# Attention over inducing points and a linearised feed-forward block: the instruction order as a table, with products and evictions moved between engines

## The chip, the cores and the metric

One core of a Trainium2 chip. The metric is device time in microseconds of one launch; the kernel before takes 184.81 us (median of 3 runs, 184.63 to 185.28). Engines: TensorE (PE; PEld is its weight load), VectorE (DVE), ScalarE (ACT), GpSimd (POOL) and SyncE (SP), whose queue issues every transfer.

## The reference

```python
def mab(q, kv):                       # x: 4 x 12480 x 128, inducing: 32 x 128, all float32
    s = (q @ kv.transpose(0, 2, 1)) / np.sqrt(C)
    s = s - s.max(-1, keepdims=True)
    a = np.exp(s)
    a /= a.sum(-1, keepdims=True) + 1e-09
    return a @ kv
h = mab(I, x)                         # 32 inducing points attend to a batch's 12480 tokens
y = mab(x, h).reshape(-1, 128)        # each token attends to the 32 rows of h
f = y @ w_in                          # 128 x 2048
out = (f - np.tanh(f)) @ w_out        # 2048 x 128
```

The inputs hold the two weights in 64 bits; the kernel brings them to 32 bits itself, from integer pieces.

## The kernel before, in words

**Batches and steps.** A batch of tokens is cut into 7 steps of 1792 tokens (the last overlaps the one before), and the steps into pairs 0-1, 2-3, 4-5 and 6. `first(b)` makes h of batch b:
- a *score step* (line 401, its matmuls on L378): four groups of 448 tokens against the inducing points, fp32, 8 matmuls. VectorE copies a pair's scores out of PSUM and takes their maximum (L405).
- the maximum over the batch (L418, L419, the product L421, L423), then per pair the exponential on ACT (L432) and a 32 x 32 block transpose on VectorE (L434).
- a *weighted sum* (L469): 14 chunks of the step against the tokens in natural layout. That layout is either loaded (`LOADED`, 13 steps of 28, L444) or made by TensorE in two *half transposes* (L454, 7 matmuls each) that ACT (L460) or VectorE (L462) copies out.
- the sums' inverse (L476 to L483), the scaling L485, and the product L487, which gives h transposed (copied by L490).

`linear(b)` replaces the feed-forward block by its tangent: h times w_in (line 505), transposed (L512), its mean over the 32 rows (L516, L517), tanh (L519), a short series of the mean on GpSimd (L525 to L530), the tangent (L535 to L539), the product with w_out (L548), and two small products (L554, L555). L561 (GpSimd) and L563 measure how far a row lies from the mean.

`second(b)` makes the outputs: scores against h (L378), the copy with the maximum (L592), one shift for each of two groups of pairs (L599 to L607), the exponential (L616), and per step an *output step* on TensorE (L631) whose two halves are evicted by ACT (L647) or VectorE (L649) and stored (L638). `bound()` (L672 to L738) decides at the end whether the tangent is good enough; if not, a general path runs, which it does not for these inputs.

**Weights.** `weight()` loads w_in and w_out in four chunks of 512 columns each (L336). A chunk takes four VectorE instructions (L339, L342, L353, L357), two on ACT (L346, L349) and a product on GpSimd (L360).

**Places.** All transfers land in 19 places of 128 x 1792 (`big`): token loads, natural layouts, weight chunks, outputs. PSUM gives three pairs of banks (`d`) for scores, transposes and outputs, and a `side` pair for small products, which one half of an output step uses too (`SIDE`).

**Order.** `Plan.add` records 584 operations with costs and priorities; `Plan.order` plays them through a list scheduler (engine costs, priorities with the hand-set offsets `JIT`, a switching cost on PE, tokens that limit how many places x and natural layouts hold) and writes the order of every engine's instructions. Evictions go to ACT or VectorE as the scheduler finds them free. On the chip each engine runs its list in that order and waits for what its next instruction needs; SyncE does so with its transfers.

Of the kernel before, what the change touches and what calls it, by code (L numbers as in the profile page):

```python
# [19 lines left out]
NQ = 4  # L20
# [16 lines left out]
JIT = {  # L37
# [28 lines left out]
}  # L66
SIDE = frozenset(((3, 3, 0),))
TOKENS = dict(x=14, nat=7)
LOADED = frozenset(((0, 6), (1, 1), (1, 2), (1, 4), (1, 6), (2, 1), (2, 3), (3, 0), (3, 1), (3, 3), (3, 4), (3, 5), (3, 6)))
RATE = 0.41  # L70
AHEAD = 5.0
LATE = 10.0
WAIT = -11.700000000000006
LOADW = (-31.5, -27.0)
PA, OT, PT, OB, PB = -8.0, 25.0, 11.0, -17.5, 16.0
LOADX, LOADN = 32, 313.5
SPLITS = ([[0, 1], [2, 3]], [[0], [1], [2], [3]], [[0, 1], [2], [3]], [[0, 1, 2, 3]], [[0, 1, 2], [3]], [[0], [1, 2, 3]])
SPLIT = (0, 4, 0, 0)
SWITCH = 12.5
PAUSE = 0.1  # L80


class Buf:


    def __init__(self, make=None, tag=None, token=None, turn=None):
        self.make, self.tag, self.token, self.turn = make, tag, token, turn
        self.t = None
        self.writer, self.readers, self.left = None, [], 0
        self.slot = None  # L90
# [7 lines left out]
class Op:  # L98
    def __init__(self, costs, fn, deps, bufs, pri, lag, size, mode):
        self.costs, self.fn, self.deps, self.bufs, self.pri, self.lag, self.size, self.mode = (  # L100
            costs, fn, deps, bufs, pri, lag, size, mode)
        self.start = self.end = self.eng = None


class Plan:


    def __init__(self, places):
        self.ops, self.places = [], places

    def add(self, eng, cost, fn, reads=(), writes=(), pri=0.0, lag=0.12, size=0, hold=(), mode=None):
        deps = set()
        for x in reads:
            if x.writer:
                deps.add(x.writer)
        for x in writes:
            if x.writer:
                deps.add(x.writer)
            deps.update(x.readers)
        costs = eng if isinstance(eng, dict) else {eng: cost}  # L120
        op = Op(costs, fn, deps, list(dict.fromkeys([*reads, *writes, *hold])), pri, lag, size, mode)
        for x in reads:
            x.readers.append(op)
        for x in writes:
            x.writer, x.readers = op, []
        for x in op.bufs:
            x.left += 1
        self.ops.append(op)
        return op

    def order(self):
        free = {tag: list(range(n)) for tag, n in self.places.items()}
        waiting, users = {}, {}
        for n, op in enumerate(self.ops):
            op.n = n
            waiting[op] = len(op.deps)
            for d in op.deps:
                users.setdefault(d, []).append(op)
        ready = {eng: [] for eng in ("ACT", "PE", "DVE", "POOL", "SP")}
        events, count = [], itertools.count()  # L140
        busy, turns = {}, {}
        mode = None
        moving = 0.0

        def release(op):
            for eng in op.costs:
                late = LATE if eng == "DVE" and len(op.costs) > 1 else 0.0
                ready[eng].append((op.pri + late, op.n, op))
                ready[eng].sort(key=lambda x: x[:2])

        for op in self.ops:
            if not op.deps:
                release(op)
        t, done = 0.0, 0
        while done < len(self.ops):
            for eng in ready:
                if busy.get(eng, -1.0) > t:
                    continue
                if eng == "SP" and moving > t + AHEAD:
                    heapq.heappush(events, (moving - AHEAD, next(count), None))  # L160
                    continue
                queue = ready[eng]
                if eng == "PE":
                    queue = sorted(queue, key=lambda x: (x[0] + (SWITCH if x[2].mode != mode else 0.0), x[1]))
                for _, _, op in queue:
                    if eng == "DVE" and len(op.costs) > 1 and busy.get("ACT", -1.0) < t + WAIT:
                        continue
                    new = [x for x in op.bufs if x.tag and x.slot is None]
                    need = {}
                    for x in new:  # L170
                        for tag in (x.tag, x.token):
                            if tag:
                                need[tag] = need.get(tag, 0) + 1
                    if any(len(free[tag]) < c for tag, c in need.items()):
                        continue
                    if any(x.turn is not None and turns.get(x.token, 0) != x.turn for x in new):
                        continue
                    for x in new:
                        x.slot = free[x.tag].pop(0)
                        if x.token:  # L180
                            free[x.token].pop()
                            turns[x.token] = turns.get(x.token, 0) + 1
# [20 lines left out]
            while events and events[0][0] <= t:  # L203
                op = heapq.heappop(events)[2]
                if op is None:
                    continue
# [16 lines left out]
def fused_kernel(ctx, tc, xT, xn, indT, w_in, w_out, outT):  # L223
# [5 lines left out]
    B = 4  # L229
# [262 lines left out]

# [357 lines left out]
```

## Time and profile before

| | |
|---|---|
| profiled execution | 184.3 us, span 182.3 us |
| PE busy | 152.7 us (84%), 1920 matmuls |
| DVE busy | 141.2 us (77%), 279 instructions |
| ACT busy | 96.0 us (53%), 141 instructions |
| POOL busy | 21.7 us (12%), 46 instructions |
| transfers | 67.76 MB, mean 372 GB/s; queue q1 93.2% of the 16 engines |

A share is an average over stages with different limits. A matmul's end is modelled, and a busy PE can be one that waits inside a group. SyncE's waits are waits of the queue's next transfer for a place or for the data it stores.

### The profile page before, as it was taken

Reading aid. Unit: us, or ns where it says so; the run is one execution under the profiler, and the core shown is the slowest. Engines: PE = TensorE matmul, PEld = TensorE weight load, DVE = VectorE, ACT = ScalarE, POOL = GpSimd, SP = SyncE. Lnnn points to the kernel's source line nnn. Section 1 sums busy time; section 2 is a strip of 40 time slices with the busy share of each in tenths; the row PEclk is TensorE's granted clock in tenths of the full one; section 3 lists DMA queues with packets and bytes.
Section 4 is the critical chain, followed back from the end, with each engine's and each line's share of the span. In section 5 each row is a group of like instructions: output and inputs, shape, how many; then the busy total and the mean of one; then the engine's idle time right before and its main releaser. Section 6 shows DMA issues by size and latency. Waiting matters only on the chain.

```text
span 182.3 us, 4643 instructions
## 1 busy us (share of the span) xinstructions
PE 152.7 (84%) x1920; PEld 85.4 (47%) x1920; DVE 141.2 (77%) x279; ACT 96.0 (53%) x141; POOL 21.7 (12%) x46
## 2 busy tenths in 40 slices
PE   0349797499999998999999999999999987899700
PEld 0019455197735574476277755535764323344200
DVE  4188999984479769788999775789988899896920
ACT  2255867841123279339435755295474752697600
POOL 1033333332005000000130000002200022000000
PEclk9999999759999999999999999999999999969955
DMA  5999999979999999899999999999999996489992
GB/s 153 348 422 425 415 410 420 373 269 337 409 423 426 414 421 333 286 422 412 368 352 419 426 416 427 418 370 350 421 419 425 423 405 276 204 351 401 400 399 75
DMA packets 11548, 67.76 MB, mean 372 GB/s; under 512 B 1408, under 2 KB 1408, under 8 KB 11520
## 3 DMA queue, kind: packets, MB, share of 16 engines
q1 hardware_dynamic: 11520, 67.39, 93.2%
q8 instruction: 17, 0.28, 0.6%
q14 instruction: 11, 0.09, 0.1%
HBM read 41.83 MB, written 25.56 MB: 370 GB/s over the span
## 4 chain that ended last, share of the span: by engine, by line
PE 69%; DVE 16%; DMA 5%; ACT 3%; issue 1%; SPq 1%; DVEq 0%; ACTq 0%
PE d L378 22%; PE side L469 14%; PE d L454 12%; PE d L631 11%; DMA big<-in_xT 5%; DVE big L649 4%; PE side L548 2%; PE side L378 2%; PE side L602 2%; ACT big L460 2%; DVE big L462 1%; DVE et L434 1%; DVE sl L405 1%; PE side L554 1%; PE side L487 1%
## 5 line engine op out<-in xcount | busy, mean ns | idle before, releaser
L647 ACT ACTIVATE big<-d,Pm,wg 128x896 f32<-128x896 f32 x28 | 30.3, 1093 | 20.4 <-PE d L631 15.5
L378 PE MATMUL d<-big,indT_sb 128*32 128x448 f32 x224 | 29.0, 586 | 12.2 <-DMA big<-in_xT 10.7
L649 DVE TENSOR_SCALAR big<-d,wg,Pm 128x896 f32<-128x896 f32 x27 | 32.5, 1204 | 3.8 <-PE d L631 2.1
L631 PE MATMUL d<-sl,k 32*128 32x448 f32 x220 | 33.3, 605 | 1.3 <-DVE all_far L563 0.8
L460 ACT COPY big<-d 128x896 f32<-128x896 f32 x22 | 19.4, 909 | 28.2 <-PE d L454 24.9
L469 PE MATMUL side<-big,et 128*32 128x128 f32 x784 | 30.7, 290 | 1.1 <-DVE et L434 1.0
L469 PEld LDWEIGHTS side<-big,et 128*32 128x32 f32 x784 | 24.9, 116 | 10.1 <-issue 4.7
L454 PEld LDWEIGHTS d<-ident,big 128*128 128x128 f32 x210 | 24.6, 149 | 10.4 <-issue 4.8
L454 PE MATMUL d<-ident,big 128*128 128x128 f32 x210 | 28.4, 289 | 0.2 <-ACT big L460 0.2
L378 PE MATMUL d<-big,hT 128*32 128x448 f32 x224 | 24.7, 542 | 0.6 <-DVE sl L592 0.6
L405 DVE TENSOR_SCALAR_CACHE_REDUCE sl<-d 128x896 f32<-128x896 f32 (+1 forms) x16 | 15.5, 970 | 5.8 <-PE d L378 5.7
L631 PEld LDWEIGHTS d<-sl,k 32*128 32x128 f32 x220 | 10.7, 187 | 15.1 <-ACT big L647 4.0
L592 DVE TENSOR_SCALAR_CACHE_REDUCE sl<-d 128x896 f32<-128x896 f32 (+1 forms) x16 | 15.4, 965 | 2.1 <-PE d L378 2.0
L434 DVE STREAM_TRANSPOSE et<-sl 128x896 f32<-128x896 f32 (+1 forms) x16 | 15.7, 984 | 1.0 <-issue 0.9
L616 ACT ACTIVATE sl<-sl,nbs 128x896 f32<-128x896 f32 (+1 forms) x16 | 15.0, 941 | 2.9 <-DVE nbs L605 2.9
L378 PEld LDWEIGHTS d<-big,indT_sb 128*32 128x32 f32 x224 | 6.9, 111 | 19.9 <-issue 10.1
L432 ACT ACTIVATE sl<-sl,nb 128x896 f32<-128x896 f32 (+1 forms) x16 | 15.0, 940 | 0.9 <-DVE nb L423 0.9
L378 PEld LDWEIGHTS d<-big,hT 128*32 128x32 f32 x224 | 7.0, 109 | 11.6 <-issue 7.0
L462 DVE COPY big<-d 128x896 f32<-128x896 f32 x8 | 8.5, 1086 | 3.0 <-PE d L454 2.3
L346 ACT ACTIVATE big<-big 128x512 f32<-128x512 uint32 x8 | 5.4, 688 | 7.6 <-DMA big<-in_w_in 7.6
L360 POOL TENSOR_TENSOR win_sb<-win_sb,big 128x512 f32<-128x512 f32 x4 | 5.6, 1392 | 18.5 <-DVE big L353 12.5
L339 DVE TENSOR_SCALAR big<-big 128x512 uint32<-128x512 uint32 x8 | 3.4, 420 | 5.2 <-DMA big<-in_w_in 5.2
(109 smaller groups left out, 136.4 us busy)
## 6 DMA issues: line engine op xcount, KB each, us to landing
big<-in_xT SPq DMA_DIRECT2D x28, 896.0 KB, 9.3
outT<-big SPq DMA_DIRECT2D x23, 896.0 KB, 6.7
big<-in_xn SPq DMA_DIRECT2D x13, 896.0 KB, 9.6
outT<-big SPq DMA_DIRECT2D x3, 864.0 KB, 9.7
big<-in_w_in SPq DMA_DIRECT2D x4, 512.0 KB, 8.4
big<-in_w_out SPq DMA_DIRECT2D x4, 512.0 KB, 14.5
outT<-big SPq DMA_DIRECT2D x3, 448.0 KB, 6.5
outT<-big SPq DMA_DIRECT2D x1, 416.0 KB, 4.7
```

What stands on the lines that cost most here:

```text
L378: nc.tensor.matmul(ps[q * m:(q + 1) * m, :n], lhsT=w, rhs=row, start=True, stop=True)
L405: nc.vector.tensor_scalar(out=sl.get()[:, :n, :], in0=ps.get()[:, :n, :W], scalar1=1.0, scalar2=None, op0=ALU.mult, op1=ALU.max, accum_out ...
L432: nc.scalar.activation(out=t, in_=t, func=AF.Exp, scale=SC, bias=nb.get(), accum_out=sums.get()[:, g:g + 1])
L434: add("DVE", 0.16 + 0.00103 * W * len(pair), lambda e, et=et, sl=sl, n=len(pair): nc.vector.transpose(out=et.get()[:, :n * KB, :].rearrang ...
L454: nc.tensor.transpose(out=o[:, k * 128:(k + 1) * 128], in_=x.get()[:, at:at + 128], identity=ident)
L460: nc.scalar.copy(out=dst, in_=src)
L469: nc.tensor.matmul(hacc.get()[q * m:(q + 1) * m, :C], lhsT=et.get()[:, j * KB + k, :], rhs=xn_t.get()[:, k * C:(k + 1) * C], start=at < NQ ...
L592: nc.vector.tensor_scalar(out=sl.get()[:, :n, :], in0=ps.get()[:, :n, :W], scalar1=1.0, scalar2=None, op0=ALU.mult, op1=ALU.max, accum_out ...
L616: nc.scalar.activation(out=t, in_=t, func=AF.Exp, scale=SC, bias=nb)
L631: nc.tensor.matmul(ds[q // 2].get()[:, q % 2, :W], lhsT=P4.get()[r, :], rhs=sl.get()[r, j, :], start=True, stop=True)
L647: nc.scalar.activation(out=dst, in_=src, func=AF.Identity, scale=wg.get(), bias=Pm.get())
L649: nc.vector.tensor_scalar(out=dst, in0=src, scalar1=wg.get(), scalar2=Pm.get(), op0=ALU.mult, op1=ALU.add)
```

## The change

The list scheduler goes. Its place takes a table, `ORDER`, of 584 words: an operation's number, the engine that runs it (P, A, D, G for GpSimd, S), and a letter for each place that it takes first. `order()` only reads it. Priorities, costs, `JIT` and tokens are gone. What differs in the instructions:
- 12 steps of natural layout are loaded instead of 13; `SIDE` has three halves instead of one.
- a weight chunk's product can run on VectorE or GpSimd; the table puts chunk 2 of w_in on VectorE, the seven others on GpSimd. L561 can run on either too: VectorE in batch 2.
- the series runs on VectorE, from the sum instead of the mean, in five instructions instead of six; the scaling of the mean (L517) goes from VectorE to ACT, and tanh scales its input itself.
- batch 1's pairs are split in two groups as 0-1, 2-3 and 4-5, 6 instead of three pairs and one.

```diff
-SIDE = frozenset(((3, 3, 0),))
+SIDE = frozenset(((3, 0, 1), (3, 3, 0), (3, 5, 1),))
-SPLIT = (0, 4, 0, 0)
+SPLIT = (0, 0, 0, 0)
+ORDER = """
+1G 2D 3D 70Sa 68Sb 97Pac 99Pb 100A 98D 75Sd 94Pae 95A 0S 20Sf 21D 4Sg 5D 7A 111Pbh 8A 69Pac 71P 6D 112D 22D 28Si 29D 24A 10D 73Sj 92Pa 9D 93A 109Pb
...
+577Pa 562S 570A 571S 578Da 579Pa 580Da 581Pa 582D 583D
+"""
     def order(self):
-        free = {tag: list(range(n)) for tag, n in self.places.items()}
...
+        for word in ORDER.split():
+            n, eng, slots = re.fullmatch(r"(\d+)([A-Z])([a-z]*)", word).groups()
+            op = self.ops[int(n)]
+            op.eng = next(x for x in op.eng.split("/") if x[0] == eng or (x, eng) == ("POOL", "G"))
+            new = [x for x in op.bufs if x.tag and x.slot is None]
+            for x, slot in zip(new, slots):
+                x.slot = ord(slot) - ord("a")
+            ops.append(op)
...
+            def scale(eng, r=r, dst=dst):
+                v = nc.gpsimd if eng == "POOL" else nc.vector
+                v.tensor_tensor(out=dst, in0=dst, in1=r["e"].bitcast(F32), op=ALU.mult)
+            add("POOL/DVE", scale, reads=[buf, ex], writes=[outs[k]])
...
+        def turned(e):
+            nc.vector.transpose(out=MT.get().rearrange("p f i -> p (f i)"), in_=psM.get())
+            nc.vector.tensor_reduce(out=total.get(), in_=MT.get(), axis=AX.X, op=ALU.add)
+        add("ACT", lambda e: nc.scalar.activation(out=th.get(), in_=total.get(), func=AF.Tanh, scale=1.0 / m),
+            reads=[total], writes=[th])
+        add("ACT", lambda e: nc.scalar.activation(out=mean.get(), in_=total.get(), func=AF.Copy, scale=1.0 / m),
+            reads=[total], writes=[mean])
         def series(e):
-            v = nc.gpsimd
+            v = nc.vector
+            a, q, y = u.get(), g.get(), total.get()
...
+            v.scalar_tensor_tensor(out=q, in0=q, scalar=c[0], in1=a, op0=ALU.add, op1=ALU.mult)
```

The table's lists, read off by engine (x12 is the token load of batch 1 step 2, n its natural layout, wi and wo chunks of w_in and w_out):

```
first transfers, before: ind x01 wi0 wi1 x00 wi2 x03 wi3 x02 x04 wo0 x05 wo1 x06 wo2 wo3 x12 n06 x10 x11 x15 x13 x14
first transfers, table:  x01 x00 x03 ind wi2 wi0 wi3 x02 x04 x05 x06 wo2 x11 x12 wo1 wi1 n05 x10 wo0 x13 wo3 x14 x15 x16
```

In the table VectorE's instructions between the last copy of batch 0's scores and the first transpose L434 are the maximum, L339 of one chunk, the shift and one copy of a half transpose; L353 and the product of chunk 2 of w_in stand ahead of that copy. After the last L487, VectorE has nine output evictions, and the part of `bound()` from L696 on stands behind the last of them; before it had eleven, and that part stood among the last four.

## Rows read from the trace of the kernel before

**Rows 1.** The page: transfer rate in 40 equal slices of the span.
```profile
GB/s 153 348 422 425 415 410 420 373 269 337 409 423 426 414 421 333 286 422 412 368 352 419 426 416 427 418 370 350 421 419 425 423 405 276 204 351 401 400 399 75
```

**Rows 2.** Busy time by stage: stage, length, PE, PEld, DVE, ACT, POOL, clock, DMA share, GB/s.
```profile
0.00:49.43 49.43, 34.55 (x395) 22.98 (x395) 35.42 (x70) 25.61 (x37) 11.93 (x15) 0.93 0.94 361
49.43:81.06 31.63, 30.79 (x443) 16.67 (x439) 25.50 (x55) 14.28 (x24) 2.59 (x9) 1.00 0.98 389
81.06:117.12 36.06, 35.70 (x481) 22.01 (x481) 30.01 (x52) 19.50 (x29) 2.35 (x7) 1.00 1.01 405
117.12:141.43 24.31, 24.13 (x372) 13.09 (x370) 21.07 (x43) 15.41 (x24) 2.47 (x8) 1.00 1.01 398
141.43:174.45 33.02, 27.56 (x240) 10.61 (x239) 29.19 (x62) 21.20 (x28) 2.35 (x7) 0.94 0.86 354
174.45:182.30 7.85, 0.00 (x0) 0.00 (x0) 0.00 (x0) 0.00 (x0) 0.00 (x0) 0.50 0.56 211
```

**Rows 3.** Instructions in time order, the first 14 us: start, duration, what, [idle before].
```profile
6.12 1.72 PE L378 MATMUL d<-big,indT_sb 128*32 128x448 f32 x8 [6.12 <-DMA big<-in_xT]
8.13 0.43 DVE L339 TENSOR_SCALAR big<-big 128x512 uint32<-128x512 uint32 x1 [5.17 <-DMA big<-in_w_in]
...
11.62 1.72 PE L378 MATMUL d<-big,indT_sb 128*32 128x448 f32 x8 [3.78 <-DMA big<-in_xT]
...
12.88 0.68 ACT L346 ACTIVATE big<-big 128x512 f32<-128x512 uint32 x1 [1.49 <-DMA big<-in_w_in]
```

**Rows 4.** The same view from 28 to 37 us.
```profile
28.72 0.69 DVE L353 SCALAR_TENSOR_TENSOR big<-big 128x512 uint32<-128x512 uint32 x1
...
29.49 1.40 POOL L360 TENSOR_TENSOR wout_sb<-wout_sb,big 128x512 f32<-128x512 f32 x1 [4.11 <-DVE big L353]
29.66 1.51 DVE L342 TENSOR_SCALAR wout_sb<-big 128x512 uint32<-128x512 uint32 x1
...
29.86 0.96 PE L378 MATMUL d<-big,indT_sb 128*32 128x448 f32 x8
...
36.48 0.87 PE L469 MATMUL side<-big,et 128*32 128x128 f32 x12 [1.01 <-DVE et L434]
```

**Rows 5.** The chain that ended last, 115 to 130 us: start, time on it, what.
```profile
118.68 1.64 PE d L378 x16
...
123.78 0.91 PE d L454 x7
...
126.44 0.96 PE d L631 x8
```

**Rows 6.** Instructions in time order around 151 us, columns as in rows 3.
```profile
150.39 1.05 POOL L561 TENSOR_TENSOR m<-m,all_mean 128x512 f32<-128x512 f32 x1
...
150.64 0.83 DVE L535 TENSOR_TENSOR all_gp<-th 128x16 f32<-128x16 f32 x1
...
152.38 0.18 DVE L538 TENSOR_TENSOR k<-all_g,k 128x16 f32<-128x16 f32 x1
```

**Rows 7.** The page: costliest groups, those of the evictions.
```profile
L647 ACT ACTIVATE big<-d,Pm,wg 128x896 f32<-128x896 f32 x28 | 30.3, 1093 | 20.4 <-PE d L631 15.5
...
L649 DVE TENSOR_SCALAR big<-d,wg,Pm 128x896 f32<-128x896 f32 x27 | 32.5, 1204 | 3.8 <-PE d L631 2.1
...
L460 ACT COPY big<-d 128x896 f32<-128x896 f32 x22 | 19.4, 909 | 28.2 <-PE d L454 24.9
...
L462 DVE COPY big<-d 128x896 f32<-128x896 f32 x8 | 8.5, 1086 | 3.0 <-PE d L454 2.3
```

**Rows 8.** Instructions in time order, VectorE from 136 us, first and last of sixteen.
```profile
165.18 0.29 DVE L696 COPY k<-side 128x128 f32<-128x128 f32 x1 [0.85 <-PE side L602]
...
173.13 0.14 DVE L738 TENSOR_SCALAR limit<-low 1x1 f32<-1x1 f32 x1
```

**Rows 9.** Who waited for whom, SyncE's queue: total us, times, longest.
```profile
SPq L393 <- PE side L469: 18.7, 7, 4.4
```

**Rows 10.** Busy time by stage, 30 to 40 us, columns as in rows 2.
```profile
30.00:40.00 10.00, 6.31 (x86) 3.76 (x85) 9.08 (x17) 7.82 (x15) 3.80 (x4) 0.70 0.91 342
```

More of the change, by code (lines that the diff above doesn't have):

```diff
@@ L98, with __init__ @@
 class Op:
[L99 to L102, printed above, removed]
+    def __init__(self, eng, fn, bufs):
+        self.eng, self.fn, self.bufs = eng, fn, bufs
 class Plan:
[L108 to L129, printed above, removed]
@@ L131, in order @@
-    def order(self):
-        free = {tag: list(range(n)) for tag, n in self.places.items()}
[L133 to L182, printed above, removed]
-                    for other in op.costs:
-                        ready[other] = [x for x in ready[other] if x[2] is not op]
-                    op.eng, op.start = eng, t
-                    busy[eng] = t + op.costs[eng]
-                    if eng == "PE":
-                        busy[eng] += PAUSE * (op.mode != mode)
-                        mode = op.mode
-                    op.end = busy[eng] + op.lag
-                    if eng == "SP":
-                        moving = max(moving, t + 1.9) + op.size / RATE
-                        op.end = moving + 1.3
-                    heapq.heappush(events, (busy[eng], next(count), None))
-                    heapq.heappush(events, (op.end, next(count), op))
-                    break
-            if not events:
-                for eng, queue in ready.items():
-                    print(eng, [(o.pri, o.n, [x.tag for x in o.bufs if x.tag and x.slot is None]) for _, _, o in queue][:6])
-                print(free, t)
-                raise SystemExit
-            t = events[0][0]
[L203 to L206, printed above, removed]
-                done += 1
-                for x in op.bufs:
-                    x.left -= 1
-                    if not x.left and x.tag:
-                        free[x.tag].append(x.slot)
-                        if x.token:
-                            free[x.token].append(None)
-                for u in users.get(op, ()):
-                    waiting[u] -= 1
-                    if not waiting[u]:
-                        release(u)
-        self.length = t
-        return sorted(self.ops, key=lambda op: (op.start, op.n))
@@ new lines, in __init__, with add @@
+    def __init__(self):
+        self.ops = []
+    def add(self, eng, fn, reads=(), writes=(), hold=()):
+        self.ops.append(Op(eng, fn, list(dict.fromkeys([*reads, *writes, *hold]))))
+    def order(self):
+        ops = []
+        for word in ORDER.split():
[3 more added lines that the diff above has]
+            new = [x for x in op.bufs if x.tag and x.slot is None]
+            assert len(new) == len(slots)
+            for x, slot in zip(new, slots):
+                x.slot = ord(slot) - ord("a")
+            ops.append(op)
+        assert len(ops) == len(set(ops)) == len(self.ops)
+        return ops
@@ L312, in constants @@
         v.memset(cols.get(), 0.0)
-    add("DVE", 1.0, constants, writes=[ones_b, cols], pri=-20)
+    add("DVE", constants, writes=[ones_b, cols])
     def make_fold(e):
@@ L321, in make_fold, with weight @@
         v.tensor_scalar(out=foldc, in0=fold2, scalar1=-1.0 / m, scalar2=None, op0=ALU.add)
-    add("DVE", 1.6, make_fold, reads=[ident_b, ones_b], writes=[fold_b], pri=-10)
-    def weight(wd, ws, outs, pri, load_pri):
+    add("DVE", make_fold, reads=[ident_b, ones_b], writes=[fold_b])
+    def weight(wd, ws, outs):
         n = 512
@@ L378, in scores, with first @@
             nc.tensor.matmul(ps[q * m:(q + 1) * m, :n], lhsT=w, rhs=row, start=True, stop=True)
-    def out_of_psum(n):
-        return {"ACT": 0.16 + 0.00084 * n, "DVE": 0.14 + 0.00105 * n}
-    def first(b, pri):
+    def first(b):
         mxg, sums = small("mxg", [128, len(PAIRS)]), small("sums", [128, len(PAIRS)])
@@ L443, in first @@
                     at = sorted(LOADED).index((b, s))
[L444 to L446 removed]
+                    add("SP", lambda e, xn_t=xn_t, at=at: nc.sync.dma_start(out=xn_t.get().rearrange("p (k c) -> p k c", c=C), in_=xn[at]),
+                        writes=[xn_t, *halves])
+                if (b, s) not in LOADED:
                     for h in range(2):
@@ L462, in out @@
                                 nc.vector.tensor_copy(dst, src)
-                        add("PE", 0.765, turn, reads=[x, ident_b], writes=[d], pri=q0 - 3 + jit("T", b, s), lag=0.2, hold=[xn_t])
-                        add(out_of_psum(HB * 128), 0, out, reads=[d, xn_t], writes=[halves[h]], pri=q0 - 3 + jit("T", b, s))
+                        add("PE", turn, reads=[x, ident_b], writes=[d], hold=[xn_t])
+                        add("ACT/DVE", out, reads=[d, xn_t], writes=[halves[h]])
                 def acc(e, et=et, xn_t=xn_t, s=s, j=j):
@@ L549, in column @@
                                  start=f < NQ, stop=f >= NF - NQ)
-        add("PE", 0.9, column, reads=[WM, *wout_b], writes=[psP], pri=pri, lag=0.2, mode="col")
-        add("ACT", 0.27, lambda e: nc.scalar.copy(out=P1.get(), in_=psP.get()[:, :128]), reads=[psP], writes=[P1], pri=pri)
+        add("PE", column, reads=[WM, *wout_b], writes=[psP])
+        add("ACT", lambda e: nc.scalar.copy(out=P1.get(), in_=psP.get()[:, :128]), reads=[psP], writes=[P1])
         def points(e):
@@ L593, in out @@
                                             op0=ALU.mult, op1=ALU.max, accum_out=bm.get()[:, at:at + 1])
-                add("DVE", 0.23 + 0.00105 * W * len(pair), out, reads=[ps, sl, *filled], writes=[part[g], bm], pri=p)
-            p = pri + PB * steps[-1] + OB
+                add("DVE", out, reads=[ps, sl, *filled], writes=[part[g], bm])
             ps = place("q")
@@ L632, in pe @@
                                              start=True, stop=True)
-                    add("PE", 0.925, pe, reads=[sl, part[g], P4], writes=ds, pri=p, lag=0.2, hold=[ot, *whole[0], *whole[1]], mode="row")
+                    add("PE", pe, reads=[sl, part[g], P4], writes=ds, hold=[ot, *whole[0], *whole[1]])
                     skip = DUP if s == NS - 1 else 0
@@ L650, in ev @@
                                                         op0=ALU.mult, op1=ALU.add)
-                        add({"ACT": 1.11, "DVE": 1.21}, 0, ev, reads=[ds[h], ot, wg, Pm], writes=[done], pri=p, hold=whole[h])
+                        add("ACT/DVE", ev, reads=[ds[h], ot, wg, Pm], writes=[done], hold=whole[h])
                         outs.append(done)
@@ L712, in least @@
             v.tensor_copy(r.get()[:, 1:2], mlarge.get())
-        add("DVE", 2.3, least, reads=[ps2, col_b], writes=[t, r], pri=pri)
+        add("DVE", least, reads=[ps2, col_b], writes=[t, r])
         def turn(e):
@@ L738, in decide @@
             v.tensor_scalar(out=limit, in0=x[:, 4:5], scalar1=-1.0, scalar2=1.0, op0=ALU.mult, op1=ALU.add)
-        add("DVE", 0.9, decide, reads=[low, *nb_b], writes=[], pri=pri)
-    weight(w_in, win_sb, win_b, 60, LOADW[0])
-    weight(w_out, wout_sb.rearrange("p f d -> p (f d)"), wout_b, 70, LOADW[1])
+        add("DVE", decide, reads=[low, *nb_b], writes=[])
+    weight(w_in, win_sb, win_b)
+    weight(w_out, wout_sb.rearrange("p f d -> p (f d)"), wout_b)
     for b in range(B):
-        P4, Pm = first(b, 100.0 * b)
-        second(b, P4, Pm, 100.0 * (b + 1))
-    bound(100.0 * B - 20)
+        P4, Pm = first(b)
+        second(b, P4, Pm)
+    bound()
     ops = plan.order()
```

227 lines of the change are left out of this document (104 added, 123 removed), and 28 rows, old and new, of the table JIT.

## The prediction

> **What bounds the kernel now.** I read the page's shares first: TensorE (PE) 84% busy, VectorE (DVE) 77%, ScalarE (ACT) 53%, and transfers that run above 400 GB/s in most slices [rows 1]. That names three candidates and decides nothing, so the stages have to be read one by one. I cut the span where TensorE ran L487, the product that completes a batch's h, at 49.43, 81.06, 117.12 and 141.43 us [rows 2]. [...] Up to the first mark it is busy 34.55 us of 49.43. After the last it is busy 27.56 of 33.02 while VectorE has 29.19, the most of any engine. The last 7.85 us are stores. So the kernel is a late start (49.4), a full middle (92.0), a tail paced by VectorE (33.0) and the last stores (7.9): 182.3 us, with 2.0 around it in this execution (184.3). The median of the runs shown, 184.81, is 0.5 above that.
>
> **Part 1, the start.** TensorE's first instruction ran at 6.12 us, on the tokens of step 1 of batch 0; the second at 11.62, on step 0's, since two weight chunks lay between [rows 3]. Transfers land one behind the other: chunk 0 is used at 8.13, step 0's tokens at 11.62, chunk 2 at 12.88. So a chunk takes 1.3 us, a token transfer 2.2 (3.5 from chunk 0 to step 0 hold one of each), and 0.7 is lost once at the start. The last tokens of batch 0 have six chunks and six token transfers between them and 6.1: 6.1 + 0.7 + 7.8 + 13.2 = 27.8 us; TensorE used them at 29.86 [rows 4]. The new list has three chunks there: 23.9.
>
> From these tokens to the first weighted sum (L469, at 36.48) VectorE is late: eight weight instructions stand in its queue from 28.72 on (two each of L353 and L342, one L357, three L339; 0.69, 1.51, by its like L353 0.69, and 0.43 us each: 6.4) [rows 3, 4], and the maximum, the shift and the transposed weights wait behind them. In the new table one L339 and one copy of a half stand there. The new chain: tokens 23.9, scores 0.9, their copy 0.7, maximum 0.4, its spreading product 0.4, shift 0.2, exponential 1.2, transpose 1.1: 28.8 us. VectorE still converts three chunks ahead of it, by its list 1.2 us more than its waits for transfers hold: 30.0 instead of 36.5. From there to L487 took 12.95; the new list has the same seven sums, less other TensorE work (10.0 in all), and twelve weight instructions on VectorE: I take 12.0, bounds 10.0 and 14.5. The first mark falls at 42.0 instead of 49.4. Not all of this is gain: by then the new list has run 9 score steps and 15 half transposes, the old 12 and 14. At 0.82 and 0.92 us [rows 5] 1.5 us of TensorE work are put off: 5.9 net.
>
> The cover: the other five chunks are now converted from 26 to 56 us, beside the first marks' TensorE work. VectorE's list from first to second mark sums to 29.2 us (25.5 busy before [rows 2]) in about 35. I add 1.0 us for it; with the cover gone it is the whole difference, 3.7.
>
> [...] The trace has L535, 16 columns wide, at 0.83 us where L538, as wide, takes 0.18; it ended at 151.47, as GpSimd's L561 did (150.39 and 1.05) [rows 6]. [...] In the new table GpSimd's product of chunk 3 becomes ready just ahead of VectorE's L353 and product of chunk 2, so these can stand for its whole 1.40 us [rows 4] ahead of the first weighted sum. I count that as a rival.
>
> **Part 2, the middle.** One step fewer is loaded: two half transposes more, 1.84 us of TensorE, for 0.92 MB, 2.2 us of a queue that isn't the bound there. By stages, from the two lists' counts. First to second mark: 3 score steps and 2 half transposes more, 1 output step (0.96) fewer, and the 1.0 of above: 31.63 + 3.3 + 1.0 = 35.9, so 77.9. Second to third: 3 half transposes fewer, 1 output step more: 36.06 - 1.8 = 34.3, so 112.2. Third to fourth: 2 half transposes more: 24.31 + 1.8 = 26.1, so 138.3, where it was 141.4.
>
> Evictions move: VectorE's 8 copies of transposes and 28 of outputs become 4 and 19, ACT's 22 and 28 become 28 and 37 [rows 7]. VectorE loses 4 x 1.09 + 9 x 1.20 = 15.2 us, ACT gains 6 x 0.91 + 9 x 1.09 = 15.3. That costs nothing while ACT is covered: its new list has some 25 of 36, 24 of 34 and 22 of 26 us in the three stages; the last, 15.41 of 24.31 before, is its thinnest cover, 4 us. [...]
>
> **Part 3, the tail.** VectorE's busy time there goes from 29.19 [rows 2] by two output evictions fewer (-2.4), by the rest of the bound, sixteen instructions from L696 to L738 [rows 8] and 4.0 us, which now stand behind the last output eviction and not ahead of it, and by the series less L517 (+0.7): 23.5. With the same idle time 27.3 us from the last mark to the last output eviction instead of 33.0, so 165.6. ACT's list there sums to 24.5 (21.20 before [rows 2]): 2.8 of cover. The last stores take 7.85 as before, and the 4.0 of the bound fit beside them. The span ends at 173.5; with the 2.0 around it 175.5; on the scale of the median 176.0. The three middle stages together hold 1.4 us in which TensorE idles; a wholly new order will have waits of its own, and I allow that sum once more: 177.4.
>
> **The rivals.**
> 1. [...] 177.4 + 1.4 = 178.8. For it the rows of L535; against it that it may fall into a wait for tokens.
> 2. *The transfers set the pace.* SyncE waited 18.7 us in seven waits for L469 to give a place free for tokens [rows 9], and there are slices of 269 to 350 GB/s [rows 1]. With the same holes in the new queue only what is no longer moved comes off: 184.8 - 2.2 = 182.6. Against it: by the sums above the tokens of batches 2 and 3 are wanted no sooner than an unbroken queue brings them.
> 3. *ACT becomes the late engine*, the slower side. In nine output steps (none before) ACT evicts both halves one behind the other: 2.2 us where TensorE took 0.96, with three pairs of PSUM banks in all, so that the next user can stand for 1.1. Nine of these are 9.9: 187.3. From the seventh that falls on the path on it is slower than 184.8. For it: the cover of 4 us in the third stage; against it: ACT still waited 15.5 us for TensorE's output steps [rows 7].
> 4. *Nothing waits*: without the allowance, with the queue's 2.2 saved among the last stores, and with part 1 anywhere in its lower half: 172 to 174.
> 5. *The lead is spent on the way*, at places that come free late: 184.8, no change, the table being only another order.
>
> **How the numbers follow.** Forecast 0.47 (177.4; its own range 174.5 to 180.5, from the bounds of part 1, -2.0 and +2.5, the cover's 2.7 and the allowance, not all at once), lock 0.12, transfers 0.13, nothing waits 0.09, no change 0.07, ACT 0.12. Faster by over 0.3% (about what a measurement of this kernel can tell from no change): 0.47 + 0.12 + 0.13 + 0.09 = 0.81; within it 0.07; slower 0.12. The range from 172 to 184 leaves out the last two, 0.19.
>
> **What would show it.** [...] Wrong: a first weighted sum after 34 (part 1); between the first and the last mark more than 4 us of TensorE idle, with ACT (rival 3) or a transfer (rival 2) ahead of it; a last stage that is still near 33 (part 3).

## The result, and the profile after

The changed kernel takes 177.91 us (median of 4 runs, 177.29 to 179.85), the kernel before 184.72 beside it: ratio 0.966, 95% interval 0.957 to 0.974. The profiled execution took 177.29, 175.7 of it span and 1.6 around it. The forecast was 177.4.

The page of the changed kernel: span, busy time, transfer rate in 40 slices, and the four groups of evictions ([rows 1, 7] before).

```profile
span 175.7 us, 4674 instructions
...
PE 146.3 (83%) x1934; PEld 85.1 (48%) x1934; DVE 126.8 (72%) x284; ACT 109.9 (63%) x160; POOL 13.8 (8%) x20
...
GB/s 202 414 411 419 421 422 411 387 362 402 423 424 400 318 376 420 367 286 405 428 397 413 428 413 421 372 341 398 419 418 421 424 421 323 417 411 412 401 259 7
...
L518 ACT ACTIVATE big<-d,Pm,wg 128x896 f32<-128x896 f32 x36 | 38.5, 1093 | 13.9 <-PE d L502 11.0
...
L341 ACT COPY big<-d 128x896 f32<-128x896 f32 x28 | 24.8, 903 | 17.9 <-PE d L335 12.9
...
L520 DVE TENSOR_SCALAR big<-d,wg,Pm 128x896 f32<-128x896 f32 x17 | 20.5, 1206 | 4.1 <-PE d L502 3.9
...
L343 DVE COPY big<-d 128x896 f32<-128x896 f32 x4 | 4.3, 1076 | 4.2 <-PE d L335 4.2
```

The sum of work is nearly what it was: 14 matmuls more, 14.4 us less on VectorE, 13.9 more on ACT, the same 1.09 and 1.20 us per eviction. TensorE is busy 6.4 us less all the same: 4.9 less in the first stage and 2.8 less in the last, where its granted clock was 0.93 and 0.94 before and is 1.00 now. What has changed is where the work stands. Busy time by stage, cut at the product that completes a batch's h (now L367) and at the end of the last output eviction, columns as in [rows 2]:

```profile
0.00:40.84 40.84, 29.64 (x378) 20.60 (x378) 28.60 (x64) 24.14 (x35) 6.71 (x12) 1.00 0.97 382
40.84:75.59 34.75, 33.01 (x470) 20.18 (x471) 27.37 (x64) 18.78 (x31) 3.81 (x5) 1.00 0.98 389
75.59:110.10 34.51, 33.11 (x467) 20.02 (x465) 23.66 (x52) 21.92 (x34) 2.22 (x3) 1.00 1.01 403
110.10:136.25 26.15, 25.26 (x386) 14.83 (x384) 21.02 (x44) 21.16 (x31) 0.00 (x0) 1.00 1.00 394
136.25:164.69 28.44, 24.75 (x240) 9.34 (x238) 22.68 (x48) 23.87 (x31) 1.05 (x1) 1.00 0.98 401
164.69:175.70 11.01, 0.51 (x4) 0.14 (x2) 3.41 (x14) 0.00 (x0) 0.00 (x0) 0.71 0.49 191
```

Read it against [rows 2], stage by stage: -8.59 at the start, +3.12, -1.55 and +1.84 in the middle, -4.58 in the last stage, and +3.16 behind the last eviction: -6.6 in all (three marks of [rows 2] stand at the product's second instruction, up to 0.17 us late; differences are good to that). Two stages gain, the middle gives back 3.4, and the end, where nothing was expected, gives back 3.2.

### The profile page after: what moved, and what is told of

The parts are those of the page before. It is cut to its first block, busy times and chain, and to the rows that moved or that the text cites. A ratio compares the mean times of both kernels' runs of the same rounds, so it can differ in the third digit from the quotient of the medians.

```text
span 175.7 us, 4674 instructions
## 1 busy us (share of the span) xinstructions
PE 146.3 (83%) x1934; PEld 85.1 (48%) x1934; DVE 126.8 (72%) x284; ACT 109.9 (63%) x160; POOL 13.8 (8%) x20
## 4 chain that ended last, share of the span: by engine, by line
PE 51%; DVE 21%; DMA 13%; ACT 8%; issue 3%; SPq 0%; DVEq 0%; ACTq 0%
PE d L265 14%; PE side L350 13%; DMA big<-in_xT 13%; PE d L502 10%; PE d L335 5%; DVE big L520 3%; DVE sl L466 3%; ACT big L518 3%; DVE et L316 2%; PE side L423 2%; ACT sl L488 2%; DVE big L240 2%; PE side L265 2%; ACT big L341 2%; PE side L475 1%
## 5 line engine op out<-in xcount | busy, mean ns | idle before, releaser
L518 ACT ACTIVATE big<-d,Pm,wg 128x896 f32<-128x896 f32 x36 | 38.5, 1093 | 13.9 <-PE d L502 11.0
L335 PE MATMUL d<-ident,big 128*128 128x128 f32 x224 | 30.8, 287 | 7.1 <-DMA big<-in_xT 6.2
L341 ACT COPY big<-d 128x896 f32<-128x896 f32 x28 | 24.8, 903 | 17.9 <-PE d L335 12.9
L502 PE MATMUL d<-sl,k 32*128 32x448 f32 x212 | 30.6, 585 | 1.9 <-ACT sl L488 1.1
L350 PE MATMUL side<-big,et 128*32 128x128 f32 x784 | 29.1, 275 | 0.3 <-ACT Pm L433 0.2
L265 PE MATMUL d<-big,indT_sb 128*32 128x448 f32 x224 | 27.3, 543 | 2.1 <-DMA big<-in_xT 2.1
L520 DVE TENSOR_SCALAR big<-d,wg,Pm 128x896 f32<-128x896 f32 x17 | 20.5, 1206 | 4.1 <-PE d L502 3.9
L343 DVE COPY big<-d 128x896 f32<-128x896 f32 x4 | 4.3, 1076 | 4.2 <-PE d L335 4.2
L436 POOL TENSOR_TENSOR m<-m,all_mean 128x512 f32<-128x512 f32 x3 | 3.1, 1048 | 52.8 <-ACT th L392 32.5
L248 POOL TENSOR_TENSOR wout_sb<-wout_sb,big 128x512 f32<-128x512 f32 x4 | 5.2, 1293 | 24.6 <-DVE big L240 19.0
```

What stands on the lines that cost most here:

```text
L265: nc.tensor.matmul(ps[q * m:(q + 1) * m, :n], lhsT=w, rhs=row, start=True, stop=True)
L335: nc.tensor.transpose(out=o[:, k * 128:(k + 1) * 128], in_=x.get()[:, at:at + 128], identity=ident)
L341: nc.scalar.copy(out=dst, in_=src)
L350: nc.tensor.matmul(hacc.get()[q * m:(q + 1) * m, :C], lhsT=et.get()[:, j * KB + k, :], rhs=xn_t.get()[:, k * C:(k + 1) * C], start=at < NQ ...
L502: nc.tensor.matmul(ds[q // 2].get()[:, q % 2, :W], lhsT=P4.get()[r, :], rhs=sl.get()[r, j, :], start=True, stop=True)
L518: nc.scalar.activation(out=dst, in_=src, func=AF.Identity, scale=wg.get(), bias=Pm.get())
```

## Experiments

All differences below are between ratios to the kernel before (which ran beside each group of runs), times its time: the changed kernel run again stands at 0.9657 (0.9587 to 0.9728). A difference under some 1.5 us is not told from none, as the base alone is known to 1.3.

**The changed kernel again**, as a base for the others.

> The changed kernel as it is, on the chip of the three runs beside it: 177.9 us (177.3 to 179.9).

178.21 us, ratio 0.9657. Marks at 41.09, 75.62, 110.13 and 136.28, last output eviction to 164.72, as in the first profile.

**The bound's chain left out.** In the changed kernel the whole chain behind L565 goes (copy, two small products, minimum, decision); the flag is set to zero at the start.

```diff
+        v.memset(limit, 0.0)
...
-        add("DVE", decide, reads=[low, *nb_b], writes=[])
+        add("DVE", lambda e: None, reads=[low, *nb_b], writes=[])
```

> Left out: the part of the bound behind the last output eviction (the copy, two small products, the minimum, the decision; 4.0 us of VectorE); the flag that the branch reads is set to zero at the start. Theory: in the changed kernel the end is no longer set by the stores but by this chain and by the branch behind it (flag written at 169.0, end of the span 6.7 later, while the last store is seen done at 171.5); without it the span ends about 1.5 us behind the last store's end, 2 to 3.3 us earlier: 175.2 us. Rival, the prediction's own: the chain fits beside the last stores, and nothing changes: 177.9, within 0.5.

174.97 us, ratio 0.948 (0.943 to 0.953): 3.3 us less. The prediction's "the 4.0 of the bound fit beside them" (the last stores) falls. In the changed kernel the chain runs from the last VectorE eviction to the flag:

```profile
162.51 1.20 DVE L520 TENSOR_SCALAR big<-d,wg,Pm 128x896 f32<-128x896 f32 x1
163.88 0.29 DVE L567 COPY k<-side 128x128 f32<-128x128 f32 x1 [0.17 <-PE side L565]
...
168.86 0.14 DVE L609 TENSOR_SCALAR limit<-low 1x1 f32<-1x1 f32 x1
```

and behind the flag every engine reads it and branches. The same kernel, the line of the branch: engine's queue, count, shortest/median/longest ns, start.

```profile
L682 ACTq COMPARE_BRANCH  x1: 50/50/50, 169.6 to 169.6; - x1
...
L682 PEldq COMPARE_BRANCH  x1: 4293/4293/4293, 169.6 to 169.6; - x1
```

TensorE's branch, 4.29 us where ACT's took 0.05, ends at 173.9; the span ends at 175.7, 6.7 us behind the flag. Before, the flag came at 173.27, ahead of the last eviction's end [rows 2, 8], and the same 5.3 us branch ran beside the last stores. The chain is hidden beside the stores only as long as flag and branch together are: the branch was in no row that the prediction looked at. The ends of the traces bear this out. In the changed kernel the span ends 1.8 us behind TensorE's branch and 4.7 behind the last packet of a store (171.05); with the bound in another order it ends 1.1 behind the branch. In the kernel before the stores come last, and the span ends 1.9 us behind their last packet (180.47); without the chain the branch ends at 173.0 and the span at 176.4.

**Nine evictions back.** The net nine evictions that ACT had gained go back to VectorE, nothing else.

```diff
-170A ... 161A ... 166A ... 192A ... 324A ... 422A ... 445A ... 450A ... 546A
+170D ... 161D ... 166D ... 192D ... 324D ... 422D ... 445D ... 450D ... 546D
```

> Nine output evictions go from ScalarE back to VectorE, so that both engines have 28 again, each at its place in the table. Three of the nine lie after the last mark. Theory: the tail is paced by VectorE, and the middle by TensorE: the marks stay (within 0.5), the last stage grows by 1.5 to 3.6 us, 179.5 to 181.5 us. Rival: ScalarE and VectorE both had room, nothing on the path: 177.5 to 178.4.

Ratio 1.014 (1.004 to 1.024), 8.9 us more than the base: slower than the kernel before, and two and a half times what I expected at most. The next two runs split it.

**Six of them, none of the last stage** (the first six words of the diff above).

> The six evictions outside the last stage go back from ACT to VectorE (02h0, 00h0, 01h1, 05h0, 16h1, 22h0); the three of the last stage stay on ACT. Nothing is left out. With all nine back the time was 188.78 against 178.21 for the changed kernel, and its stages from the second mark on grew by 1.3, 4.5, 1.8 and 3.1 us. Theory (the middle has no cover on VectorE: a PSUM pair waits behind VectorE's other work and TensorE behind the pair): about 7 us of the 10.6 are these six, 185, with the growth between the first and the fourth mark. Rival (the prediction's part 2: six times 1.2 us more on VectorE fit beside TensorE's work): under 179.5, and the 10.6 were nearly all the tail's.

184.83 us, ratio 1.002 (0.997 to 1.008): 6.7 us more; the rival, that the middle is free, falls. The three middle stages of this run, and who made TensorE (PE) and its weight load (PEld) wait in them for VectorE's output evictions (total us, times, longest):

```profile
40.60:76.43 35.83, 33.87 (x471) 20.34 (x471) 28.30 (x65) 17.19 (x30) 3.80 (x5) 1.00 0.92 366
76.43:113.34 36.91, 33.55 (x467) 19.94 (x466) 25.70 (x54) 20.80 (x32) 2.22 (x3) 1.00 0.99 392
113.34:141.48 28.14, 25.71 (x385) 14.68 (x384) 23.24 (x46) 18.22 (x28) 0.00 (x0) 1.00 0.96 373
```

```profile
PE d L335 <- DVE big L520: 1.5, 1, 1.5
PE d L502 <- DVE big L520: 1.4, 2, 1.2
...
PEld d L502 <- DVE big L520: 3.7, 3, 2.0
PEld d L335 <- DVE big L520: 1.8, 1, 1.8
```

The changed kernel has one such wait between the same marks:

```profile
PEld d L502 <- DVE big L520: 0.7, 1, 0.7
```

VectorE is busy 23 to 28 us of 28 to 37, so it has time; but an eviction stands in its queue behind copies and transposes, its pair of banks stays taken, and TensorE, which has three pairs in all, stands. TensorE's idle time in the middle goes from 4.0 to 7.8 us, its busy time from 91.4 to 93.1, and the stages grow by 5.5. "Beside other work" was judged by totals, where the place in the queue decides.

**Three of them, the last stage's** (the last three words).

> Only the three evictions of the last stage (25h1, 26h1, 33h0) go back from ACT to VectorE; nothing is left out. Theory: the last stage alone grows, by up to three times 1.20 us: 3.0, so 181.2, with the marks where they were (41, 75.6, 110.1, 136.3). Rival 1 (it has slack on VectorE: 22.7 busy of 28.3): under 179. Rival 2 (one displaced eviction sets off a row of waits, and the 10.6 us are the tail's): over 185.

180.83 us, ratio 0.983 (0.976 to 0.989): 3.1 us more, as the theory has it. The two parts sum to 9.8, the nine together cost 8.9.

**Two weight chunks loaded ahead.** Chunks 2 and 1 of w_out are loaded before two token transfers of batch 0; conversions stay where they are.

```diff
-73Sj ... 78Sk ... 52Sp ... 44Ss
+52Sp 73Sj ... 44Ss 78Sk
```

> The loads of two w_out chunks stand ahead of the tokens of steps 2 and 4 of batch 0, as five chunks and not three stood there; all else as in the changed kernel. Theory: the start is paced by the arrival of batch 0's last tokens, and the full middle carries a late start to the end undiminished: first weighted sum 2.6 us later (31.8), every mark 2.6 later, 180.5 us. Rival: VectorE's conversions pace the start, or the middle has slack that takes it up: first weighted sum less than 1 us later, 178.0 to 178.6.

179.0 us, ratio 0.971 (0.966 to 0.977): 1.0 us more, not told from none. In its profile the last tokens of batch 0 are used at 25.16 (23.97 in the changed kernel), the first weighted sum is at 30.36, the first mark at 42.03: 1.2 us late, less than two chunks at 1.3, as part of the loading time falls into waits that were there. That is neither the theory's 2.6 nor the rival's less than 1.

**The same two chunks, converted ahead of the maximum.** As the run above, and the 14 conversion words of the two chunks stand ahead of the word of batch 0's maximum (87D), so that eight such VectorE instructions stand there. In the old order four of its eight [rows 4] stood ahead of the maximum (L418 at 32.24) and four between it and the first transpose, so this run goes further than the old order did.

> The changed kernel with two weight chunks (2 and 1 of w_out) loaded ahead of two token transfers of batch 0, and with their whole conversion moved in the queues of VectorE, ACT and GpSimd ahead of batch 0's maximum; all else as it was, nothing left out. The loads alone had put the first weighted sum 0.9 us later, at 30.36. Theory (the prediction's part 1: VectorE's queue ahead of the maximum is on the path): VectorE's eight instructions of the two chunks, 2 x (0.42 + 0.43 + 0.69 + 0.69) = 4.5 us, come on top: first weighted sum near 34.8, first mark near 45, and since the same work is then missing behind it, the end later by 2 to 4.5 us. Rival (the late end is the tokens' alone): first weighted sum near 30.4 and no more than 1 us over the run with the loads alone.

184.97 us, ratio 1.003 (0.999 to 1.006): 6.8 us more than the base, level with the kernel before. Spoiling the start alone takes the whole gain back; as moving six evictions back does so too, the losses of the single runs are not shares of the gain. Its first stage and 8 us of it by busy time, and then instructions in time order:

```profile
0.00:48.44 48.44, 32.33 (x377) 22.56 (x378) 28.37 (x64) 22.59 (x33) 7.14 (x12) 0.93 0.80 313
...
30.00:38.00 8.00, 5.17 (x28) 3.74 (x32) 6.04 (x9) 4.65 (x9) 2.93 (x3) 0.64 0.25 105
```

```profile
31.74 1.04 DVE L301 TENSOR_SCALAR mq<-mask,mx 128x4 f32<-128x4 f32 x1
...
32.84 0.59 PE L303 MATMUL side<-mq,fold 128*128 128x4 f32 x2 [5.83 <-DVE mq L301]
...
37.94 2.25 PE L350 MATMUL side<-big,et 128*32 128x128 f32 x56
```

L301 stands at 31.74 where the changed kernel has 25.94. Of these 5.8 us the loads alone are 1.2 (27.13 in the run before this one) and the conversions 4.6, near the 4.5 of my sum. What the sum had not was behind L301. It took 1.04 us, not 0.23, beside GpSimd's products. TensorE had stood 5.83 us, and its granted clock was 0.64 over those 8 us, in which transfers ran at 105 GB/s, where it was 1.00 over the ten before. From L301 to the first weighted sum it is 6.2 us, where the changed kernel and the run before this one have 3.2, so that sum is not at 34.8 but at 37.94. The later stages are those of the changed kernel (34.61, 34.50, 26.15, 28.42, 10.98): a late start is handed through to the end undiminished.

**The moved product back on GpSimd.** Only the product of chunk 2 of w_in.

```diff
-27D
+27G
```

> Only the product of chunk 2 of w_in goes from VectorE to GpSimd (as in the kernel before, where GpSimd did all eight); nothing is left out. In the changed kernel this VectorE product took 1.66 us beside GpSimd's of chunk 3, and VectorE then still waited 1.15 us for the last scores. Theory (the product falls into the wait for tokens): within 0.4 us of the changed kernel's time. [...]

177.68 us, ratio 0.963 (0.958 to 0.968): 0.5 less, within the error; the time alone could hardly tell the 1.4 us of the prediction's first rival from none, but the trace can. The two products do take longer side by side, and that cost nothing. Instructions in time order in the changed kernel:

```profile
20.70 1.67 POOL L248 TENSOR_TENSOR win_sb<-win_sb,big 128x512 f32<-128x512 f32 x1 [3.18 <-DVE win_sb L244]
...
21.26 1.66 DVE L248 TENSOR_TENSOR win_sb<-win_sb,big 128x512 f32<-128x512 f32 x1
...
23.97 0.96 PE L265 MATMUL d<-big,indT_sb 128*32 128x448 f32 x8 [2.07 <-DMA big<-in_xT]
...
25.08 0.62 DVE L289 TENSOR_SCALAR_CACHE_REDUCE sl<-d 128x448 f32<-128x448 f32 x1 [1.15 <-PE d L265]
...
29.17 1.08 PE L350 MATMUL side<-big,et 128*32 128x128 f32 x32
```

Both products take 1.66 us side by side, where GpSimd's takes 1.29 with VectorE idle beside it (at 35.86), and a VectorE product of that shape 0.69 (L414, further below). But VectorE still waits 1.15 us for the last scores, which wait 2.07 for their tokens.

**The series back on GpSimd**, in six instructions.

```diff
-            v = nc.vector
+            v = nc.gpsimd
...
-            v.scalar_tensor_tensor(out=q, in0=q, scalar=c[0], in1=a, op0=ALU.add, op1=ALU.mult)
+            v.tensor_scalar(out=q, in0=q, scalar1=c[0], scalar2=None, op0=ALU.add)
+            v.tensor_tensor(out=q, in0=q, in1=a, op=ALU.mult)
```

> The series of each batch runs on GpSimd again, in six instructions, with all else as in the changed kernel; nothing is left out. [...] Theory (hidden in three batches, on the path in the last): 178.2 + about 1 = 179. [...] Rival 2 (each batch's tangent comes late and the second phase with it): 182.

176.86 us, ratio 0.965 (0.958 to 0.972): no difference. In the last batch the column product (of the tangent with w_out, L548 in the kernel before) comes 8.6 us behind the mark, 8.3 in the changed kernel. My theory of 1 us there is not borne out; the move is free either way, within the error.

**The bound in another order.** The parts that need no product of the chain run while TensorE does the chain's products; eight small VectorE instructions leave the way to the flag.

```diff
-            v.tensor_copy(r.get()[:, 1:2], mlarge.get())
+            nc.tensor.transpose(out=ps4.get()[:1, :128], in_=mlarge.get(), identity=ident)
...
-577Pa 562S 570A 571S 578Da 579Pa 580Da 581Pa 582D 583D
+584Pb 577Pa 562S 570A 571S 578Da 579Pa 585D 580Da 581Pa 586D 582D 583D
```

> The same bound computed in another order; nothing is left out. The parts that need no product of the last chain (the slack from the maxima, the test of the largest mean with a transpose of its own) run while TensorE does the chain's short products, so that eight small VectorE instructions leave the chain from the last output eviction to the flag (L583, L596, L597, L604 to L607, 0.13 to 0.27 us each with their gaps, and one memset). Theory (the chain and the branch behind it set the end): flag and end 1.5 us earlier, 176.6; without the chain at all it was 174.97. Rival (the stores behind the last evictions, done by 171.5 of 175.7, hold it): no more than 0.3 us.

177.58 us, ratio 0.967 (0.962 to 0.972): no gain. In its profile the flag stands 4.4 us behind VectorE's last eviction, not 5.3, but reading it took twice as long. Reading the flag, VectorE's queue:

```profile
L691 DVEq TENSOR_LOAD <-limit x1: 1125/1125/1125, 169.5 to 169.5; - x1
```

(0.54 us in the changed kernel.) Four of its six runs had spans of 174.1 to 174.6 us, under the base's best of 175.3, and 2.8 to 3.4 us around them instead of 1.5 (the run with the product on GpSimd has 1.9 to 3.7). What that time holds no view shows; it stays open.

**Evictions of the tail alone, in the old order.** The kernel before with three VectorE evictions of its last stage on ACT, and, in the second run, with the bound's chain behind the last eviction as well.

```diff
+    for k in ((2, 6, 1), (2, 5, 1), (3, 3, 0)):
+        EV[k].eng = "ACT"
...
+    ops = [op for op in ops if op not in CHAIN] + [op for op in ops if op in CHAIN]
```

> The kernel before, with its old order, and three output evictions of its last stage moved from VectorE to ACT: (2,6) half 1, (2,5) half 1, (3,3) half 0. Nothing is left out. Theory (VectorE paces the last stage, and an output eviction there is worth its 1.2 us): faster by 2 to 3.6 us. Rival (ACT is late as soon as it takes them, or the old order waits elsewhere): within 0.6 us of the kernel before.

> As the run beside it (the kernel before with three evictions of its last stage on ACT), and the bound's chain (four VectorE and two TensorE steps of 4.0 us) put behind the last output eviction; nothing left out. Theory from the run without the chain (flag to end 6.7 us, last eviction to flag 4.2): the last output eviction comes up to 4 us earlier, and the end follows it by 10.9 and not by 7.85: 1 us less than the run beside it. Rival 1 (the chain fits beside the last stores, as the prediction had it): 4 us less. Rival 2 (it was in VectorE's idle time): no less, or up to 3 more.

184.64 us, ratio 1.002 (0.998 to 1.005), and 187.04, ratio 1.011 (1.005 to 1.016). Both theories fall: the evictions bring nothing, and the chain behind the end costs 1.7 more. Last stage of the first run, and what VectorE and ACT did in it (this profiled execution, 186.16 us, is the slowest of its twelve):

```profile
142.01:176.43 34.42, 29.50 (x242) 11.62 (x240) 26.27 (x59) 24.21 (x31) 2.70 (x7) 0.90 0.83 339
```

```profile
151.57 1.00 DVE L538 TENSOR_TENSOR k<-all_g,k 128x16 f32<-128x16 f32 x1 [0.31 <-POOL all_g L530]
...
153.11 2.09 ACT L648 ACTIVATE big<-d,Pm,wg 128x896 f32<-128x896 f32 x2 [1.15 <-PE d L632]
...
156.67 0.29 DVE L606 TENSOR_REDUCE nbs<-side 128x1 f32<-128x128 f32 x1 [1.98 <-ACT k L557]
```

VectorE has 2.9 us less to do than in [rows 2] and the stage is 1.2 longer. One eviction fewer stands ahead of the last batch's tangent, but the column product comes only 0.7 earlier behind the mark: VectorE now waits 0.31 for GpSimd's series, and L538 takes 1.00 beside GpSimd's L561, where in the kernel before L535 took 0.83 beside it. Then VectorE waits 1.98 for ACT's small copy L557, which stood behind two evictions, 2.09 us. Of the lead 0.2 us is left at the bound's 32 matmuls (L694, here L695). From there on it is TensorE's granted clock, which falls in both kernels, but here for longer. Two stretches of the kernel before, two of this run, then those matmuls in both:

```profile
161.00:164.60 3.60, 3.60 (x44) 1.95 (x40) 3.29 (x5) 3.60 (x4) 0.00 (x0) 0.61 0.84 339
164.60:168.00 3.40, 3.24 (x30) 1.47 (x22) 2.24 (x6) 2.47 (x5) 0.00 (x0) 1.00 1.02 416
...
162.00:165.50 3.50, 3.31 (x36) 1.79 (x36) 1.57 (x4) 3.50 (x5) 0.00 (x0) 0.50 0.75 300
165.50:169.00 3.50, 3.50 (x28) 1.68 (x22) 1.27 (x3) 2.14 (x4) 0.00 (x0) 0.71 0.90 365
```

```profile
163.55 1.17 PE L694 MATMUL side<-big,cols 128*32 128x128 f32 x32
164.12 1.93 PE L695 MATMUL side<-big,cols 128*32 128x128 f32 x32 [0.19 <-ACT big L648]
```

In the second run VectorE has 6.4 us less to do, and the stage (here up to the bound's first copy) is 0.8 shorter:

```profile
140.91:173.16 32.25, 27.01 (x236) 10.20 (x234) 22.81 (x43) 24.31 (x31) 2.71 (x7) 0.95 0.84 344
```

VectorE's busy time did not pace the old last stage. What VectorE alone was worth there is not measured, as both runs load ACT with three evictions in exchange.

## Why the prediction was right, and where it was not

| step | forecast | measured |
|---|---|---|
| last tokens of batch 0 used | 23.9 | 23.97 |
| first weighted sum | 30.0 | 29.17 |
| L367, four times | 42.0, 77.9, 112.2, 138.3 | 40.84, 75.59, 110.10, 136.25 |
| last output eviction ends | 165.6 | 164.69 |
| from there to the span's end | 7.85 | 11.01 |
| ACT busy (96.0 + 15.3 forecast) | 111.3 | 109.9 |

**The start** was right in mechanism and size: -8.6 forecast as -7.4, and the granted clock does not fall in it: 1.00 over the stage, where [rows 10] have 0.70. Of the 1.2 us more, 0.8 are the conversions ahead of the sum, which fell into the waits for tokens. The two runs with weight chunks ahead show the mechanism: conversion in VectorE's queue ahead of the maximum is worth far more than the loads (6.8 us for both, 1.0 for the loads alone).

**The middle** was right in size (96.3 forecast, 95.4 measured), by errors that nearly cancel. TensorE's busy time grew by 0.8 us (90.6 to 91.4), where the sum has 3.3 and 1.0 more for the cover; its idle time is 4.0 us, where it was 1.4 and the allowance would make it 2.8. So new waits did come. They are mostly for VectorE's small steps around the end of a batch's h and in its tangent:

```profile
PE side L423 <- DVE nbs L478: 1.2, 1, 1.2
PE side L429 <- DVE rs L362: 0.9, 1, 0.9
PE side L475 <- DVE k L365: 0.8, 1, 0.8
```

ACT has a small copy among them (L433, 0.7), but neither its evictions nor a transfer made TensorE's matmuls wait there, so the sign against part 2 (over 4 us idle with one of them ahead) did not come, though the 4 us did. TensorE stays the bound. But "that costs nothing while ACT is covered" told half of it. The move is what lets TensorE stay the bound: with six of the evictions back the new order loses 6.7 us. The sum came out since the evictions were on ACT, and I had no price for what it would be otherwise. Rival 3, that ACT becomes late, fell here (it waited 11.0 us for TensorE's output steps); in the old order, with three evictions more in the tail, ACT's copy L557 came to stand behind two of them.

**The last stage** came out as 28.4 against 27.3, by reasons that do not hold. The step that failed is "with the same idle time 27.3 us". The forecast is 23.5 us of VectorE's work and 3.8 idle; measured are 22.7 and 5.8. (By the trace VectorE has twelve output evictions behind the mark before and nine after, three fewer and not two.) No run shows the forecast's +0.7 us for the series less L517 as a difference of times; the traces have the series' five instructions at 0.17 to 0.18 us each in the changed kernel (0.88 in all, 140.33 to 141.35), and L517 at 0.17 in the kernel before. Busy time taken from VectorE was booked as time taken from the stage, and in the old order taking 2.9 us from it took nothing, and 6.4 took 0.8. What the trace shows instead is a place in a queue. In the kernel before, three output evictions stand in VectorE's queue ahead of the last batch's tangent, and the column product follows 12.1 us after L487 (its first instruction, at 141.26; [rows 2] cuts at its second):

```profile
142.70 1.21 DVE L649 TENSOR_SCALAR big<-d,wg,Pm 128x896 f32<-128x896 f32 x1
...
146.58 1.21 DVE L649 TENSOR_SCALAR big<-d,wg,Pm 128x896 f32<-128x896 f32 x1 [0.18 <-issue]
...
149.51 1.21 DVE L649 TENSOR_SCALAR big<-d,wg,Pm 128x896 f32<-128x896 f32 x1
...
153.34 1.08 PE L548 MATMUL side<-wout_sb,m 128*32 128x128 f32 x32 [1.02 <-DVE m L539]
```

In the changed kernel one stands there, and the product comes 8.3 us after the mark:

```profile
137.75 1.21 DVE L520 TENSOR_SCALAR big<-d,wg,Pm 128x896 f32<-128x896 f32 x1 [0.50 <-PE d L502]
...
143.80 0.69 DVE L414 TENSOR_TENSOR m<-m,k 128x512 f32<-128x512 f32 x1
144.54 1.08 PE L423 MATMUL side<-wout_sb,m 128*32 128x128 f32 x32 [0.27 <-DVE m L414]
```

That is 3.8 of the 4.7 us that the stage has become shorter, counted from the product's first instruction in both. Ahead of the column product VectorE has two evictions fewer (2.4 us by their length) and one copy of scores fewer (L592, 1.1), and the series (1.0) more; the rest are shorter waits, and the successor of L535 takes 0.44 for 0.83. No run changed that place alone, and the runs near it price an eviction there lower. With three back in the new order (3.1 us) one more stands there, and the product comes 9.0 us after the mark, 0.7 later; with all nine back two more, and 1.4 later; with one fewer there in the old order it came 0.7 earlier, which ACT and the clock then lost. So an eviction there is worth about 0.7 us at the product. From the product to the last eviction it is 1.0 us less (20.1 for 21.1). In that part TensorE's granted clock fell before (0.61 from 161.0 to 164.6) and does not fall in the changed kernel (1.00 over the stage); no run tells this from what the order does there, and how the whole splits stays open.

**The end** is the mis-sized term: 11.01 for 7.85. The chain of the bound does not fit beside the stores, since behind its flag come 6.7 us of reading, branch and close. The run without the chain has the price, 3.3 us.

So the total was right by a balance: 1.2 better at the start, 0.9 better in the middle, 1.1 and 3.2 worse in the tail and at the end, and 1.4 of allowance on top. That the parts nearly cancel is luck. Rivals 1 and 2 fell (in the first, "lock" among the chances, VectorE's longer product fell into a wait for tokens; the transfers still have slices of 286 to 318 GB/s, but TensorE and its weight loads waited 0.2 us for tokens from the first mark on); rival 4's "nothing waits" fell with the 4.0 us of the middle. No run undoes the other parts of the change alone (one loaded step fewer, `SIDE`, `SPLIT`, L561 on VectorE in batch 2), so what each of them is worth is not known.

## What to carry to other kernels

Where one engine bounds the middle, as here, a late start goes through to the end one for one (7.6 us late at the first mark and 7.4 at the span's end, in the run with the conversions ahead): look first at what stands in each queue ahead of the first product of the bound engine. Price an eviction by what stands ahead of it in its queue and by who waits for its PSUM pair, not by its engine's share of the stage: the same three evictions were worth 3.1 us in one order and nothing in the other. And when the work behind the last transfer moves, look at what the program does after its last result: here what follows a flag that every engine reads (6.7 us) was longer than the chain that computes it (5.3).

## What the runs showed of the hardware

- A branch over a long body that is not run took 0.05 to 0.07 us on four engines. On TensorE it took 4.29 us in the changed kernel, 5.30 in the kernel before, 4.39 with the bound in another order and 5.74 without the chain. In the changed kernel seven packets of the instruction queues (q8 and q14) run during its 4.29; what TensorE waited for no run shows.
- Reading one word into five engines' registers took 0.47 to 0.54 us in the changed kernel, where the core's transfers moved 330 GB/s beside it, and 1.08 to 1.15 in the kernel before, where they moved 387 to 395. With the bound in another order it took 1.03 to 1.13, without the chain 0.88 to 1.17. No run changed the transfers alone.
- A VectorE instruction of 4 columns took 1.04 us beside GpSimd's products and 0.23 without; one of 16 columns 1.00 beside GpSimd's L561 and 0.18 without. What makes them longer no run shows.
- In the run with the conversions ahead the granted clock of TensorE was 0.64 over the 8 us in which a wait of 5.83 us ended, and the eight matmuls of a score step took 1.72 us there, in place of 0.96. The early wait cost 3.0 us more than itself: 6.2 from L301 to the first weighted sum in place of 3.2, of which L301's own length is 0.8.
